# Loading two weight matrices through casting DMAs from GpSimd instead of staged loads and engine casts, with batch 1's loads held back by a gate

## The chip, the core and the metric

The kernel runs on one core of a Trainium2 chip. The metric is the device time of one execution in microseconds (us), given as the median of several runs. The engines are TensorE (PE, with its weight loads as PEld), VectorE (DVE), ScalarE (ACT), GpSimd (POOL) and SyncE (SP, which here only issues DMAs). Each engine works through its own instructions in order and waits for others by semaphores. Sixteen DMA engines move data between HBM and SBUF.

## The reference

A retention layer over eight batches (batch 8, heads 8, sequence 576, head size 64) is followed by a two-layer network with a tanh-gelu. All inputs and the output are float32.

```python
scores = (1 / sqrt(64)) * q @ k.transpose(0, 1, 3, 2)
gamma = 1 - 2.0 ** (-5 - arange(H))
Dmat = where(rel >= 0, gamma ** rel, 0)          # rel = row position - column position
x = (scores * Dmat) @ v                          # then to [4608 tokens, 512]
h = x @ w_in                                     # w_in  512 x 2048
g = 0.5 * h * (1 + tanh(sqrt(2 / pi) * (h + 0.044715 * h**3)))
out = g @ w_out                                  # w_out 2048 x 512
```

## The kernel before

The work is cut into token blocks of 512 (`TB`), nine of them: one for each batch's first 512 positions, and a last block that gathers the remaining 64 positions of all eight batches. All matmuls have float16 operands. For each batch there is an attention part (transposes, scores, masks, running states, outputs) that leaves `xT`, and a network part on `xT`: `up` matmuls with `w_in_sb` into PSUM, the gelu on ScalarE into `gT`, and `prod` matmuls with `w_out_sb` and with sums of its quarters (`wt`, made by VectorE at L764). The order of all instructions is written out by hand: the emission order in the program is each engine's order, and `at(t, u, f)` hangs a piece of work `f` on step `u` of block `t`. Negative steps of block 0 lie in its `up` part. While block 0's network part runs, batch 1's attention is slotted in, and so on.

At the start, batch 0's twelve loads of q, k and v go through SP into ten staging buffers (`lds`, float32, 128 by 512 each, freed by `unstage`). `cc` casts a staged tile to float16 on a chosen engine, frees its buffer, and calls `pump`, which issues the next loads in the list `seq` as long as buffers are free. An entry `("h",)` in `seq` stops `pump` until `resume` is called.

After batch 0 the list holds 16 loads of `w_in` (L121) and 16 of `w_out` (L126), each 256 KB, and then batch 1's loads. `w_in` comes in four column groups of 512 in the order `QS = (0, 2, 1, 3)`, each as four chunks of 128 rows (`ct`); `w_out` in sixteen chunks of 128 rows. `cast_w` (its cast is L921) casts the staged chunks into `w_in_sb` and `w_out_sb`: all of `w_in` and chunks 0 to 9 of `w_out` on GpSimd, chunks 10 to 15 on ScalarE (`BY_ACT`).

PE's order at the start is: batch 0's attention; `up_halves` on column group 0; the rest of batch 0's outputs; then fourteen more `up_half` steps of eight matmuls each (L614), groups 0 and 2 first and then 1 and 3; then the products of block 0 (L802): product 1 (opA, w_out chunks 0 to 7), product 5 (opC), product 2 (opA again, chunks 8 to 11 and then 12 to 15), products 3, 6, 7 and 4 with batch 1's attention among them. Batch 1's casts of q and k for the first half run on VectorE (L292), of v on GpSimd (L280); its q is turned at step 8 of block 0.

Of the kernel before, what the change touches and what calls it, by code (L numbers as in the profile page):

```python
# [20 lines left out]
def kernel(  # L21
# [9 lines left out]
    nc = tc.nc  # L31
# [8 lines left out]
    NF = DF // 128  # L40
# [20 lines left out]
    def bank(name, dt=F32):  # L61
        n = spare.popleft()
        t = ps.tile([128, 512 if dt == F32 else 1024], dt, tag=f"p{n}", name=name, bufs=1)
        home[id(t)] = (n, t)
        return t

    def drop(t):
        spare.append(home.pop(id(t))[0])
# [4 lines left out]
    def lds(name="ld", shape=(128, 512), dt=F32):  # L73
        n = stage.popleft()
        t = sb.tile(list(shape), dt, tag=f"ld{n}", name=name, bufs=1)
        staged[id(t)] = (n, t)
        return t

    def unstage(t):
        if id(t) in staged:  # L80
            stage.append(staged.pop(id(t))[0])
# [19 lines left out]
    def load(b, key, c):  # L101
        src = SRC[key]
        t = lds()
        if b < NPE or key == "q":
            g, y = c // 2, c % 2
            nc.sync.dma_start(
                out=t.rearrange("p (n x) -> p n x", n=4),
                in_=src[b, y::2, 256 * g : 256 * g + 256, :].rearrange("n (p j) d -> p n (j d)", j=2),
            )
        else:  # L110
            nc.sync.dma_start(
                out=t.rearrange("p (h d) -> p h d", d=D),
                in_=src[b, :, 128 * c : 128 * c + 128, :].rearrange("h s d -> s h d"),
            )
        att[b]["raw"][key, c] = t

    w_raw = {}

    def load_w_in(g, ct):
        t = lds()  # L120
        nc.sync.dma_start(out=t, in_=moe_w_in[128 * ct : 128 * ct + 128, 512 * g : 512 * g + 512])  # L121
        w_raw["i", g, ct] = t

    def load_w_out(f):
        t = lds()
        nc.sync.dma_start(out=t, in_=moe_w_out[128 * f : 128 * f + 128, :])  # L126
        w_raw["o", f] = t

    def parts(b):
        if b == NPE:  # L130
            return [(key, c) for key in "kqv" for c in range(NC)]
        return [(key, c) for c in range(NC) for key in "kqv"]

    def body(b):
        if b < NPE:
            return [("b", b, key, 2 * g + y) for g in range(2) for key in "qkv" for y in range(2)]
        return [("b", b, *x) for x in parts(b)]

    QS = (0, 2, 1, 3)
    seq = body(0) + [("i", g, ct) for g in QS for ct in range(4)]  # L140
    seq += [("o", f) for f in range(NF)] + body(1)
    TP = {4: 0, 5: 2, 6: 4, 7: 6}
    for b in range(1, B):
        seq += body(b) if b > 1 else []
# [6 lines left out]
    def pump():  # L151
        while q_ld["next"] < len(seq) and not q_ld["hold"]:
            s = seq[q_ld["next"]]
            if s[0] == "h":
                q_ld["hold"] = True
                q_ld["next"] += 1
                return
            if s[0] != "t":
                if not stage:
                    return  # L160
            q_ld["next"] += 1
            {"b": load, "i": load_w_in, "o": load_w_out, "t": load_tails}[s[0]](*s[1:])

    pump()


# [22 lines left out]
    for n in range(2):  # L189
# [3 lines left out]
            out=lp[:, 32 + 16 * n : 48 + 16 * n].rearrange("p (x h) -> p x h", h=8),  # L193
# [50 lines left out]
    w_in_sb = const.tile([128, 4, DF], F16, name="w_in_sb")  # L244
    w_out_sb = const.tile([128, NF, DM], F16, name="w_out_sb")
# [3 lines left out]
    def filler(n, w=512):  # L249
        t = bank("fill")  # L250
        for _ in range(n):
            for x in range(0, 512, w):
                nc.tensor.matmul(t[:, x : x + w], ident, wide[:, x : x + w], start=(x == 0), stop=True, skip_group_check=True)
        drop(t)
# [17 lines left out]
    def cast(b, key, c, eng):  # L272
        a = att[b]
        raw = a["raw"].pop((key, c))
        dst = a[key][:, 512 * c : 512 * c + 512]
        if key == "v":
            if eng is nc.scalar:
                eng.copy(out=dst, in_=raw)  # L278
            else:
                eng.tensor_copy(out=dst, in_=raw)  # L280
        elif key == "q" and NPE <= b < PAIR:
            g, y = c // 2, c % 2
            for x in range(2):
                eng.tensor_tensor(  # L284
                    out=a[key][:, 1024 * g + 512 * x : 1024 * g + 512 * x + 512].rearrange("p (n l d) -> p l n d", l=2, d=D)[:, y ^ x],
                    in0=raw[:, 256 * x : 256 * x + 256].rearrange("p (n d) -> p n d", d=D),
                    in1=sp[key][:, 4 * x : 4 * x + 4, y].unsqueeze(2).to_broadcast([128, 4, D]),
                    op=ALU.mult,
                )
        elif b < NPE:  # L290
            y = c % 2
            eng.tensor_tensor(  # L292
                out=a[key][:, 1024 * (c // 2) : 1024 * (c // 2) + 1024].rearrange("p (n l d) -> p l n d", l=2, d=D)[:, y],
                in0=raw.rearrange("p (n d) -> p n d", d=D),
                in1=sp[key][:, :, y].unsqueeze(2).to_broadcast([128, 8, D]),
                op=ALU.mult,
            )
        else:
            s0 = {"q": 0, "k": 2}[key] + (b >= PAIR)
            dh, rh = (x.rearrange("p (h d) -> p h d", d=D) for x in (dst, raw))  # L300
            for o, i in ((slice(0, 4), slice(0, 4)), (slice(4, 8, 2), slice(5, 8, 2)), (slice(5, 8, 2), slice(4, 8, 2))):
                x = rh[:, i]
                eng.tensor_tensor(  # L303
                    out=dh[:, o], in0=x, in1=sc[:, s0, i].unsqueeze(2).to_broadcast(list(x.shape)), op=ALU.mult
                )
# [31 lines left out]
    def resume():  # L337
        q_ld["hold"] = False
        pump()
# [185 lines left out]
    def past2(b, c):  # L525
        xs = bank("xs")
        att[b]["xs", c] = xs
        if c > 0:
            for p in range(HP):
                nc.tensor.matmul(  # L530
                    xs[:, 128 * p : 128 * p + 128], tbd[b % 2][:, c - 1, p, :], tq(b, c, p),
                    start=(p == 0), stop=True, skip_group_check=True,
                )
# [371 lines left out]
            drop(op.pop("B"))  # L905
            send(keep["o1"], 1)

    CP = {"i": 0, "o": 0}

    def cast_w(kind, *i):  # L910
        src = w_raw.pop((kind,) + i)
        if kind == "i":
            g, ct = i
            dst = w_in_sb[:, ct, 512 * g : 512 * g + 512]
        else:
            dst = w_out_sb[:, i[0], :]
        n = CP[kind]
        late = kind == "o" and n in BY_ACT
        eng = nc.scalar.copy if late else nc.gpsimd.tensor_copy
        CP[kind] += 1  # L920
        eng(out=dst, in_=src)  # L921
        unstage(src)
        pump()

    HALF = (2, 6)
    BY_ACT = range(10, 16)

    def cc(b, key, c, eng):
        raw = att[b]["raw"][key, c]
        cast(b, key, c, eng)  # L930
        unstage(raw)
        pump()
# [4 lines left out]
    def later(b, c, cp=None):  # L937
        scan(b, c) if b < NPE else scan_halves(b, c, cp=cp or A.copy)
        spread(b, c, cp or A.copy)
# [19 lines left out]
    for x in range(2):  # L959
        masks2(0, 0, x)  # L960
        if x == 0:
            later(0, 0)
    cc(0, "q", 2, P), cc(0, "q", 3, P)
    cc(0, "k", 2, P), cc(0, "k", 3, V)
    cc(0, "v", 2, A), cc(0, "v", 3, P)
    filler(6)
    past2(0, 0), past2(0, 1)
    av2(0, 0)
# [8 lines left out]
    for x in range(2):  # L977
        masks2(0, 1, x)
        if x == 0:
            later(0, 2)  # L980
    for g in QS:
        for ct in range(4):
            cast_w("i", g, ct)
    up_halves(0, 0, (0, 2))
    past2(0, 2), past2(0, 3)
    av2(0, 1)
# [6 lines left out]
    def at(t, u, f, last=False):  # L993
        events.setdefault((t, u, last), []).append(f)
# [22 lines left out]


    at(0, -12, lambda: V.memset(tbd[1][:, 1:], 0.0))
    for f in range(NF):  # L1020
        at(0, (f - 10) // 2 if f in BY_ACT else -7 + f // 2 if f < 8 else -1, lambda f=f: cast_w("o", f))
    for u, f, ns in ((-4, 0, (0,)), (-1, 4, (0,)), (2, 0, (1, 2)), (4, 4, (1, 2))):
        at(0, u, lambda f=f, ns=ns: weight_sums(f, ns, V))
    for u, f, e in ((6, 0, V), (6, 4, V)):
# [106 lines left out]
    for t in range(1, B):  # L1131
        b, tl = t + 1, TP.get(t)
# [12 lines left out]
    for b in range(NPE, B):  # L1145
        ent = parts(b)
        eng = {"k": P, "q": P, "v": P if b == NPE + 1 else A}
# [121 lines left out]
```

## Time and profile before

| | |
|---|---|
| runs shown, us | 282.88, 284.13, 284.18 (median 284.13) |
| profiled execution, us | 283.43 |
| its span, us | 281.7 |
| TensorE clock granted | 0.997 of full |
| PE, DVE, ACT, POOL busy, us | 271.3, 234.8, 170.4, 137.3 |
| read from and written to HBM, MB | 36.70, 9.44 |
| w_in load, issue to landing, us (median) | 5.9 |
| w_out load, issue to landing, us (median) | 5.3 |

The profile is of one execution. Its span runs from the first to the last instruction; the time of the execution holds 1.7 us more. Timeline lines give start, duration, engine, line, operation, output and input, a count where like instructions are merged, and in brackets the idle time before and what ended it. Rows by stage give for each engine its busy time and count of instructions, then the granted TensorE clock, the mean busy share of the DMA engines and GB/s. "SPq" is SP's queue of DMA issues.

### The profile page before, as it was taken

To read this page: it belongs to the slowest core of one execution; us is meant where nothing else is said; L and a number is where in the kernel's file an instruction comes from. 1 tells how busy PE (TensorE), PEld (TensorE's weight loads), DVE (VectorE), ACT (ScalarE), POOL (GpSimd) and SP (SyncE) were. 2 spreads that over 40 slices of the span, in tenths; PEclk is the share of its full clock that TensorE was granted. 3 is DMA by queue.
4 is the path that set the end of the run, shared out by engine and by line. 5 is a ranking of instruction groups with operands and counts; after the bars stand their busy time and mean duration, and the time that the engine had idled before them with its cause. 6 is when DMAs were issued, how large, how long until landed. Compare 5 with 4: busy or idle time off the path is not lost.

```text
span 281.7 us, 9782 instructions
## 1 busy us (share of the span) xinstructions
PE 271.3 (96%) x4106; PEld 214.2 (76%) x4106; DVE 234.8 (83%) x441; ACT 170.4 (60%) x325; POOL 137.3 (49%) x239
## 2 busy tenths in 40 slices
PE   6789999999999999999999999999999999999994
PEld 3458887888877688768876886688668887887783
DVE  6784999998979799779988997889798977975874
ACT  5377755797336864785468745884587358407810
POOL 5579909890596089108961797169817000000000
PEclk9999999999999999999999999999999999999998
DMA  6999999999998994999699989999992240003005
GB/s 187 304 376 341 388 307 259 232 198 243 248 221 156 284 223 95 258 239 238 126 199 282 210 186 189 282 212 195 193 269 44 40 153 1 2 31 120 0 7 144
DMA packets 127307, 54.11 MB, mean 192 GB/s; under 512 B 93472, under 2 KB 119072, under 8 KB 127264
## 3 DMA queue, kind: packets, MB, share of 16 engines
q1 hardware_dynamic: 126672, 52.97, 77.3%
q8 instruction: 32, 0.52, 0.8%
q10 hardware_dynamic: 592, 0.52, 0.5%
q14 instruction: 11, 0.09, 0.1%
HBM read 36.70 MB, written 9.44 MB: 164 GB/s over the span
## 4 chain that ended last, share of the span: by engine, by line
PE 70%; DVE 13%; DMA 6%; ACT 4%; POOL 3%; issue 2%; SPq 1%; DVEq 0%
PE hp L593 11%; PE opB L802 11%; PE opA L802 10%; PE opC L802 8%; PE hB L695 8%; PE opD L802 4%; DMA ld<-in_moe_w_in_dram 4%; PE hC L695 4%; PE xs L428 3%; PE hp L614 3%; DVE wt L764 2%; ACT gT L710 2%; DMA ld<-in_v_dram 2%; POOL w_in_sb L921 2%; PE hA L695 2%
## 5 line engine op out<-in xcount | busy, mean ns | idle before, releaser
L802 PEld LDWEIGHTS <-gT 128*128 128x128 f16 x576 | 55.0, 98 | 8.7 <-issue 0.2
L593 PE MATMUL hp<-xT,w_in_sb 128*128 128x512 f16 x192 | 49.1, 379 | 0.0
L802 PEld LDWEIGHTS <-s 128*128 128x128 f16 x432 | 42.0, 98 | 5.1
L303 POOL TENSOR_TENSOR ck<-ld,sc 128x128 f16<-128x128 f32 (+1 forms) x72 | 43.3, 628 | 2.9 <-DMA ld<-in_k_dram 2.5
L599 ACT ACTIVATE gT<-hp 128x512 f16<-128x512 f32 x48 | 28.5, 594 | 11.0 <-PE hp L593 10.9
L802 PE MATMUL opA<-w_out_sb,gT 128*128 128x256 f16 x288 | 35.0, 273 | 0.0
L284 POOL TENSOR_TENSOR cq<-ld,sc 128x256 f16<-128x256 f32 x48 | 32.1, 690 | 0.0
L695 PEld LDWEIGHTS <-w_in_sb 128*128 128x128 f16 x256 | 25.1, 98 | 8.2
L614 PE MATMUL hp<-xT,w_in_sb 128*128 128x256 f16 x256 | 29.8, 273 | 1.5 <-POOL w_in_sb L921 1.3
L614 PEld LDWEIGHTS <-w_in_sb 128*128 128x128 f16 x256 | 24.2, 98 | 5.8 <-POOL w_in_sb L921 2.8
L593 PEld LDWEIGHTS <-w_in_sb 128*128 128x128 f16 x192 | 18.7, 98 | 12.8 <-DVE xT L579 0.2
L710 ACT ACTIVATE gT<-k 128x512 f16<-128x512 f32 x25 | 15.8, 632 | 13.1 <-DVE k L706 13.1
L695 PEld LDWEIGHTS <-wi 128*128 128x128 f16 x192 | 18.3, 98 | 5.2
L621 ACT ACTIVATE gT<-hp 128x512 f16<-128x512 f32 x32 | 18.5, 599 | 4.8 <-PE hp L614 4.7
L1157 POOL COPY gate<-s 128x1 f16<-128x1 f16 x5 | 2.5, 496 | 38.4 <-DVE s L777 30.9
L776 DVE TENSOR_TENSOR s<-gT 128x512 f16<-128x512 f16 (+1 forms) x26 | 14.7, 566 | 7.7 <-ACT gT L621 5.0
L579 ACT CAST xT<-xs 128x512 f16<-128x512 f32 x23 | 15.3, 734 | 8.7 <-PE xs L428 8.7
L695 PE MATMUL hC<-x,w_in_sb 128*128 128x256 f16 x128 | 19.2, 273 | 0.0
L695 PE MATMUL hB<-x,wi 128*128 128x256 f16 x128 | 18.9, 273 | 0.0
L802 PE MATMUL opB<-wt,gT 128*128 128x256 f16 x144 | 18.2, 273 | 0.0
L278 ACT CAST cv<-ld 128x512 f16<-128x512 f32 x22 | 13.7, 622 | 7.4 <-DMA ld<-in_v_dram 7.4
L779 DVE TENSOR_TENSOR gT<-gT 128x512 f16<-128x512 f16 (+1 forms) x26 | 18.1, 712 | 0.0
(150 smaller groups left out, 569.3 us busy)
## 6 DMA issues: line engine op xcount, KB each, us to landing
ld<-in_q_dram SPq DMA_DIRECT2D x32, 256.0 KB, 5.6
ld<-in_k_dram SPq DMA_DIRECT2D x32, 256.0 KB, 5.7
ld<-in_v_dram SPq DMA_DIRECT2D x32, 256.0 KB, 5.6
out_dram<-ost SPq DMA_DIRECT2D x16, 512.0 KB, 4.7
ld<-in_moe_w_in_dram SPq DMA_DIRECT2D x16, 256.0 KB, 5.9
ld<-in_moe_w_out_dram SPq DMA_DIRECT2D x16, 256.0 KB, 5.3
lt<-in_k_dram SPq DMA_DIRECT2D x8, 128.0 KB, 5.9
lt<-in_q_dram SPq DMA_DIRECT2D x8, 128.0 KB, 4.5
```

Source lines behind the costliest of these rows:

```text
L284: eng.tensor_tensor(out=a[key][:, 1024 * g + 512 * x : 1024 * g + 512 * x + 512].rearrange("p (n l d) -> p l n d", l=2, d=D)[:, y ^ x], in ...
L303: eng.tensor_tensor(out=dh[:, o], in0=x, in1=sc[:, s0, i].unsqueeze(2).to_broadcast(list(x.shape)), op=ALU.mult)
L579: cp(out=xT[:, g0 : g0 + 4 : 2].rearrange("p g n (t j) -> p g n j t", j=2), in_=t.rearrange("p (n g j t) -> p g n j t", n=HP, g=2, j=2),)
L593: nc.tensor.matmul(hp.rearrange("p (g t) -> p g t", t=TL), w_in_sb[:, ct, 128 * fc : 128 * fc + 128], xT[:, o : o + TB // TL, ct, :], star ...
L599: nc.scalar.activation(out=gT[t][:, fc].rearrange("p i n -> p (i n)"), in_=hp, func=AF.Gelu_apprx_tanh)
L614: nc.tensor.matmul(hps[n][:, 256 * x : 256 * x + 256].rearrange("p (g t) -> p g t", t=TL), w_in_sb[:, ct, 128 * (fs[n] + x) : 128 * (fs[n] ...
L621: nc.scalar.activation(out=gT[t][:, f : f + 2, 2 * u : 2 * u + 2, :].rearrange("p f i n -> p f (i n)"), in_=hp.rearrange("p (f n) -> p f n ...
L695: nc.tensor.matmul(pb[:, 256 * i : 256 * i + 256].rearrange("p (g t) -> p g t", t=TL), w(kt, i), x(kt), start=(new and i == kt == 0), stop ...
L710: due.append(lambda: nc.scalar.activation(out=g, in_=x.rearrange("p (f n) -> p f n", f=2), func=AF.Gelu_apprx_tanh))
L776: nc.vector.tensor_tensor(out=s["1"], in0=a21, in1=a22, op=ALU.add)
L779: nc.vector.tensor_tensor(out=a21, in0=a11, in1=a21, op=ALU.subtract)
L802: nc.tensor.matmul(op[tag][:, HD * u : HD * u + HD], lhs(f), rhs[:, f], start=(new and f == 0), stop=(f == NH - 1), skip_group_check=True,)
```

## The change

Both weight matrices are no longer staged. Nine DMAs issued from GpSimd read the float32 weights from HBM and write float16 straight into `w_in_sb` and `w_out_sb`: group 0 of `w_in` in two halves of 512 KB, the other three groups in 1 MB each, and `w_out` in four quarters of 1 MB. The issues stand in GpSimd's order among batch 0's second-half casts. All 32 staged weight loads on SP, and the 26 casts on GpSimd and six on ScalarE, are taken out.

Batch 1's loads now follow batch 0's in `seq`, behind a hold that is lifted at step -9 of block 0. The first of them must wait for a new one-column copy on GpSimd, which reads chunk 11 of `w_out` (the last of its third quarter) and writes into the buffer that this load fills. In the built program the copy waits for the eighth of the nine DMAs, and the ninth DMA waits for the first, whose semaphore it uses again.

```diff
     def load(b, key, c):
         t = lds()
+        if (b, key, c) == (1, "q", 0):
+            nc.gpsimd.tensor_copy(out=t[:, 0:1], in_=w_out_sb[:, 11, 0:1])
...
-    def load_w_in(g, ct):
-        t = lds()
-        nc.sync.dma_start(out=t, in_=moe_w_in[128 * ct : 128 * ct + 128, 512 * g : 512 * g + 512])
-        w_raw["i", g, ct] = t
-
-    def load_w_out(f):
-        t = lds()
-        nc.sync.dma_start(out=t, in_=moe_w_out[128 * f : 128 * f + 128, :])
-        w_raw["o", f] = t
+    def load_w_in(g, c0, c1):
+        nc.gpsimd.dma_start(
+            out=w_in_sb[:, c0:c1, 512 * g : 512 * g + 512],
+            in_=moe_w_in[128 * c0 : 128 * c1, 512 * g : 512 * g + 512].rearrange("(c p) f -> p c f", p=128),
+        )
+
+    def load_w_out(f0, f1):
+        nc.gpsimd.dma_start(
+            out=w_out_sb[:, f0:f1], in_=moe_w_out[128 * f0 : 128 * f1, :].rearrange("(f p) d -> p f d", p=128)
+        )
...
-    seq = body(0) + [("i", g, ct) for g in QS for ct in range(4)]
-    seq += [("o", f) for f in range(NF)] + body(1)
+    seq = body(0) + [("h",)] + body(1)
...
     cc(0, "q", 2, P), cc(0, "q", 3, P)
+    load_w_in(0, 0, 2)
     cc(0, "k", 2, P), cc(0, "k", 3, V)
+    load_w_in(0, 2, 4)
     cc(0, "v", 2, A), cc(0, "v", 3, P)
+    load_w_in(2, 0, 4)
+    load_w_in(1, 0, 4)
+    load_w_in(3, 0, 4)
+    load_w_out(0, 4)
+    load_w_out(4, 8)
+    load_w_out(8, 12)
+    load_w_out(12, 16)
     filler(6)
...
-    for g in QS:
-        for ct in range(4):
-            cast_w("i", g, ct)
     up_halves(0, 0, (0, 2))
...
-    for f in range(NF):
-        at(0, (f - 10) // 2 if f in BY_ACT else -7 + f // 2 if f < 8 else -1, lambda f=f: cast_w("o", f))
+    at(0, -9, resume)
```

`cast_w`, `BY_ACT` and `w_raw` are removed with their uses.

More of the change, by code (lines that the diff above doesn't have):

```diff
@@ L115, in load @@
         att[b]["raw"][key, c] = t
-    w_raw = {}
-    def load_w_in(g, ct):
-        t = lds()
-        nc.sync.dma_start(out=t, in_=moe_w_in[128 * ct : 128 * ct + 128, 512 * g : 512 * g + 512])
-        w_raw["i", g, ct] = t
-    def load_w_out(f):
-        t = lds()
-        nc.sync.dma_start(out=t, in_=moe_w_out[128 * f : 128 * f + 128, :])
-        w_raw["o", f] = t
+    def load_w_in(g, c0, c1):
[7 more added lines that the diff above has]
+        )
     def parts(b):
@@ L161, in pump @@
             q_ld["next"] += 1
-            {"b": load, "i": load_w_in, "o": load_w_out, "t": load_tails}[s[0]](*s[1:])
+            {"b": load, "t": load_tails}[s[0]](*s[1:])
     pump()
@@ L906, in after @@
             send(keep["o1"], 1)
[L908 to L923, printed above, removed]
     HALF = (2, 6)
-    BY_ACT = range(10, 16)
     def cc(b, key, c, eng):
```

## The prediction

> **What bounds the kernel now.** I read the page's busy shares first, then the busy time by stage, then the timeline of the start and the waits there.
>
> ```profile
> span 281.7 us, 9782 instructions
> ...
> PE 271.3 (96%) x4106; PEld 214.2 (76%) x4106; DVE 234.8 (83%) x441; ACT 170.4 (60%) x325; POOL 137.3 (49%) x239
> ```
>
> TensorE (PE) is busy in 96% of the span, so 10.4 us of idle time are all that better loading could win. The stages show where they are.
>
> ```profile
> core 0: us, PE busy (x) PEld busy (x) DVE busy (x) ACT busy (x) POOL busy (x), PEclk, DMA share, GB/s
> ...
> 12.30:16.50 4.20, 3.54 (x119) 2.63 (x119) 3.64 (x8) 3.14 (x8) 1.59 (x2) 1.00 1.08 355
> 16.50:22.00 5.50, 4.08 (x60) 2.52 (x61) 4.08 (x9) 3.60 (x8) 5.11 (x8) 1.00 1.05 374
> 22.00:34.00 12.00, 12.00 (x111) 10.75 (x112) 8.37 (x12) 8.66 (x17) 11.65 (x17) 1.00 1.01 362
> 34.00:41.70 7.70, 7.70 (x73) 6.88 (x71) 7.60 (x14) 4.87 (x9) 1.47 (x2) 1.00 1.13 320
> 41.70:50.70 9.00, 8.36 (x174) 7.17 (x173) 8.93 (x16) 5.25 (x7) 7.42 (x9) 1.00 1.05 249
> ```
>
> After 22 us PE is full, but for 0.64 us at 41.7 to 50.7, where batch 1's attention is slotted in. The weights stream from about 12 to 38 us with the 16 DMA engines saturated (share 1.0 or more) at 362 to 374 GB/s. In 16.5 to 22.0 PE waits for weights:
>
> ```profile
> 10.13 11.66 SPq L121 DMA_DIRECT2D ld<-in_moe_w_in_dram  x16
> ...
> 12.23 1.05 POOL L292 TENSOR_TENSOR ck<-ld,sc 128x512 f16<-128x512 f32 x1
> ...
> 14.69 0.61 POOL L280 CAST cv<-ld 128x512 f16<-128x512 f32 x1 [1.41 <-DMA ld<-in_v_dram]
> ...
> 16.55 5.33 POOL L921 CAST w_in_sb<-ld 128x512 f16<-128x512 f32 x8 [1.25 <-DMA ld<-in_moe_w_in_dram]
> ...
> 17.22 1.28 PE L614 MATMUL hp<-xT,w_in_sb 128*128 128x256 f16 x8 [0.76 <-POOL w_in_sb L921]
> ...
> 20.83 0.78 PE L614 MATMUL hp<-xT,w_in_sb 128*128 128x256 f16 x3
> ...
> 21.93 8.25 PE L614 MATMUL hp<-xT,w_in_sb 128*128 128x256 f16 x74 [0.33 <-POOL w_in_sb L921]
> ```
>
> The eight casts at 16.55 are column groups 0 and 2 of w_in. PE starts at 17.22 on the first, follows them chunk by chunk, and only from 21.93 runs without a stop. Its work from 16.5 to 21.93 is 19 matmuls of L614 at 0.109 us (0.87 us for eight) and 1.1 us of attention, 3.2 us in 5.4: about 2.2 us are lost here. That and the 0.64 us are the ceiling of any gain.
>
> ```profile
> 33.25 1.13 SPq L106 DMA_DIRECT2D ld<-in_q_dram  x2
> ...
> 33.84 1.91 PE L802 MATMUL opA<-w_out_sb,gT 128*128 128x256 f16 x16
> ...
> 37.37 1.91 PE L802 MATMUL opA<-w_out_sb,gT 128*128 128x256 f16 x16
> ```
>
> These set the later deadlines: in chunks of 128 rows, the first opA needs chunks 0 to 7 of w_out, the second chunks 8 to 11 at 37.37 and 12 to 15 eight matmuls later, at 38.24. Batch 1's first load leaves SP at 33.25.
>
> **What goes.** 26 casts on POOL (16 of w_in, median 0.62 us, and ten of w_out, median 0.80) and six on ACT (0.62) fall away. PE waited only for the first eight, priced below; the rest ran beside a full PE, so they are worth nothing in themselves. VectorE's sums beside them take 0.71 to 0.83 us (L777 to L781) and 0.42 once POOL is quiet, but VectorE there waits for gelus. SP loses 32 issues and 8.4 MB of staged loads.
>
> **What comes: the issues.** GpSimd issues in order, so nine issues of cost c stand in its queue: one between the casts of q3 and k2, one between k2 and v3, seven behind v3. No row shows a DMA issued from POOL. Nearest below: SP's w_in issue of 128 rows, 0.33 us at the least. From above: SP's longest batch-0 or batch-1 q issue (512 rows, as in seven of the nine), 1.34 us. A cost below zero is excluded, since POOL must at least step through the instruction. I take 0.8 us, between the two and equal to POOL's own median for a w_out cast. k2 then ends at 13.28+0.8 = 14.1 (PE turns k at 14.10, so it hardly notices), v3 at 15.5 in place of 15.3 (PE's state matmuls want it at 16.0). At c = 1.34 v3 ends at 16.6, and PE's attention is 0.6 us late.
>
> In one sentence of its own: the Trainium skill (DMA: Bandwidth & Descriptors, Latency and other measured facts) gives about 1 us to the first byte for a GpSimd DMA against 0.6 for one of SP, which no run here shows yet, and by an estimate from it each landing would be 0.4 us later.
>
> **The transfers.** I take the old stream's rate, 370 GB/s of float32 read: 1 MB in 2.83 us. Landing after the last byte: batch 0's first load, issued at 0.81 into an idle queue, released VectorE at 3.85; less 0.46 of issue and 0.7 of transfer that leaves 1.8 us. With c = 0.8: group 0's halves flow from 13.1 and 14.9 and land at 16.3 and 18.2; group 2 is issued by 16.3 and lands at 21.0. Before, PE had 3 of its 8 matmuls done when it resumed at 21.93, as if it had started at 21.6. So 0.6 us are won here (1.3 us at c = 0.33; 1.0 us lost at 1.34). Groups 1 and 3 land at 23.8 and 26.7, wanted at 26.2 and 28.0. The quarters of w_out land at 29.5, 32.3, 35.2 and, undisturbed, 38.0; PE wants them at 33.2, 33.2, 36.8 and 37.6. VectorE's weight sums (L764) began at 30.93, 34.91, 37.39 and 38.72, one for each quarter, so they too meet their data but for the last.
>
> The last is late. The gate opens at 35.2 and batch 1's loads then share the engines with the last quarter: at half rate for it, 38.9. PE stops 1.3 us there, and 0.6 won becomes 0.7 lost.
>
> **The gate.** The one-column copy waits on POOL for w_out chunk 11. Behind it there stand only batch 1's casts of v, q and k, whose data it holds back anyway; on SP all of batch 1's loads stand behind q's first. Before, these began at 33.25 and took until 43.7 (SP waited for staging buffers); now ten go without a buffer wait from 35.3. Into the shared engines, q lands at 38.8 and 39.5, k at 40.2 and 40.9, v at 41.6 and 42.3; before, with 5.5 us from issue to landing, 38.8, 39.4, 40.3 and so on, v released POOL at 42.23. VectorE's casts of q began at 40.05. So batch 1 is at most some tenths late. Of the 0.7 us, 0.2 vanish into PE's 0.64 us of idle time.
>
> **Sum.** The profiled execution took 283.43 us (span 281.7 and 1.7 around it); +0.5 gives 283.9. The median of the runs shown is 284.13, 0.7 above it, so on that scale 284.6. About 0.5%, 1.4 us, is what a measurement of this kernel can tell from no change.
>
> **Rivals.**
>
> *Converting in flight is slower than copying* (25%). Nothing in the trace converts inside a DMA. For it: the engines are already saturated at 370 GB/s, and the last quarter has no slack (38.0 against 37.6), so every loss of rate reaches PE. Against it: the bytes read are the same and those written are half. It decides from a rate of about 355 GB/s, where 8.4 MB take 1 us longer. At 90% the stream is 2.5 us longer (287), at 75% 7.6 us (292), at half rate 22.7 us (307).
> The Trainium skill (DMA: Bandwidth & Descriptors, Bandwidth, Measured) lists 341 GB/s for 1 MB from GpSimd; by an estimate from that the stream takes 24.6 us in place of 22.7 and the sum is 1.9 us higher, 286.5. The old stream's 374 GB/s is from SP, so the trace neither agrees nor disagrees.
>
> *The issues are dear* (18%): c at 1.34 us or more, or a first issue of several us. Place: POOL between q3 and v3. All landings move by three issues, 1.6 us at c = 1.34: w_out's last quarter at 40.5, 2.3 us late; 286 to 287. It decides from c = 1.1.
>
> *Faster* (20%): issues of 0.33 us and a stream above 400 GB/s because half as much is written. Group 2 lands before 20.0, PE resumes 1.5 us or more earlier, and w_out's last quarter, 2 us earlier, no longer stops it: 282.0 to 282.7. The ceiling of 2.2+0.64 us speaks against much more. For it: 18 us of POOL's casts really are gone, and PE waited 4.1 us for them by the waits:
>
> ```profile
> PEld L614 <- POOL w_in_sb L921: 2.8, 6, 0.9
> ...
> PE hp L614 <- POOL w_in_sb L921: 1.3, 3, 0.8
> ```
>
> (weight loads and matmuls count the same stops twice.) Against it: those casts ran almost as fast (0.62 us for 256 KB) as the transfers do (0.71 us), so what replaces them is the DMA's own pace.
>
> *No change beyond 1.4 us* (37%) is the forecast. That the gate does not hold is excluded: q's load writes the column that the copy writes, so it must follow it.
>
> **The numbers.** Near zero 0.37, slower 0.43 (25+18), faster 0.20. The faster case reaches down to 282.0. Upward the range takes the dear issues and the milder half of the slow stream, to 84% of its rate (4.3 us on top of 0.5), 289; beyond lie about 13%.
>
> **What would show it.** Right: PE's unbroken run of L614 begins near 21.0; a POOL issue takes 0.5 to 1.1 us; a short stop at the second opA; batch 1's q casts begin at 40 to 40.5; everything after 60 us is as before but shifted. Wrong: DMA busy with less than 340 GB/s from 15 to 36 us, or PE waiting for w_out by several us (slow stream); k2's cast after 15 us (dear issues); w_out's third quarter before 33 us (faster).

## The result and the profile after

The changed kernel takes 285.20 us (median of nine runs, 284.92 to 287.72), the kernel before, beside it and over nine runs, 283.52: a ratio of 1.0065, 95% interval 1.0040 to 1.0091. That is 1.8 us slower by the ratio, past the 0.5%, 1.4 us, that the prediction named as what can be told from no change. The profiled execution took 285.1 us, of which 283.4 are span (before: 283.43 and 281.7).

From the page after: the span, the engines' busy times and the two DMA queues that matter (packets, MB, share of 16 engines).

```profile
span 283.4 us, 9700 instructions
...
PE 271.6 (96%) x4106; PEld 215.2 (76%) x4106; DVE 231.3 (82%) x441; ACT 167.4 (59%) x319; POOL 125.6 (44%) x223
...
q1 hardware_dynamic: 122064, 44.58, 68.8%
q0 software_dynamic: 4240, 4.19, 9.3%
```

PE's work is the same (271.6 us against 271.3), VectorE and GpSimd have 3.5 and 11.7 us less to do, and the span is longer all the same. The software queue's 4.19 MB are the float16 bytes written of both weights. So where it alone is at work, the GB/s of the stages below are written bytes, and the float32 read is twice that.

Busy time by stage, after:

```profile
core 0: us, PE busy (x) PEld busy (x) DVE busy (x) ACT busy (x) POOL busy (x), PEclk, DMA share, GB/s
...
12.30:16.50 4.20, 3.19 (x90) 2.31 (x94) 4.03 (x6) 2.69 (x6) 4.18 (x6) 1.00 0.75 133
16.50:22.00 5.50, 3.56 (x68) 2.74 (x56) 4.59 (x10) 2.93 (x7) 4.08 (x6) 0.85 0.95 136
22.00:34.00 12.00, 11.55 (x129) 10.15 (x128) 4.42 (x11) 8.35 (x16) 0.00 (x0) 0.93 1.24 207
34.00:41.70 7.70, 7.70 (x73) 6.90 (x72) 6.26 (x14) 2.81 (x6) 0.19 (x1) 1.00 0.99 215
41.70:50.70 9.00, 8.92 (x177) 7.77 (x174) 8.28 (x15) 4.25 (x6) 5.92 (x7) 1.00 1.12 274
```

From 22 to 34 us the new stream runs at 207 GB/s written, 414 read, faster than the old one's 362. From 16.5 to 22 us it runs at 136 written, some 270 read, where the old one had 374. The stage before, with 133 in place of 355, still holds the last of batch 0's plain loads. PE's idle time moved with that: 1.94 us in 16.5 to 22.0 (before 1.42) and 0.45 in 22 to 34 (before none), while 41.7 to 50.7 is nearly full (8.92, before 8.36). PEclk is 0.85 and 0.93 in the two stages, so some of PE's busy time there is work at half speed.

GpSimd's timeline after shows the issues (L120, L126) and the gate (L105):

```profile
12.15 0.89 POOL L120 DMA_DIRECT2D w_in_sb<-in_moe_w_in_dram  x1
...
14.06 0.76 POOL L120 DMA_DIRECT2D w_in_sb<-in_moe_w_in_dram  x1
...
15.37 2.24 POOL L120 DMA_DIRECT2D w_in_sb<-in_moe_w_in_dram  x3
17.59 2.99 POOL L126 DMA_DIRECT2D w_out_sb<-in_moe_w_out_dram  x4
36.48 0.19 POOL L105 CAST ld<-w_out_sb 128x1 f32<-128x1 f16 x1 [15.91 <-issue]
```

An issue takes 0.75 to 0.89 us. PE's timeline after:

```profile
16.87 1.03 PE L614 MATMUL hp<-xT,w_in_sb 128*128 128x256 f16 x8
19.85 1.42 PE L614 MATMUL hp<-xT,w_in_sb 128*128 128x256 f16 x8 [1.94 <-DMA w_in_sb<-in_moe_w_in_dram]
...
23.57 12.49 PE L614 MATMUL hp<-xT,w_in_sb 128*128 128x256 f16 x112 [0.45 <-DMA w_in_sb<-in_moe_w_in_dram]
35.89 1.91 PE L802 MATMUL opA<-w_out_sb,gT 128*128 128x256 f16 x16
...
39.39 1.91 PE L802 MATMUL opA<-w_out_sb,gT 128*128 128x256 f16 x16
```

The first eight matmuls run at 16.87, as soon as the first half is there. Then PE stands for 1.94 us for the second half, and the unbroken run begins at 23.57 on group 2, where the kernel before had an equivalent start of 21.6. Both opA steps are 2.0 us later than before (33.84, 37.37). Neither stops for w_out.

One row per us, in the same columns, shows the slow stretch (the trace's landing records give group 0's halves at 16.4 and 19.8, group 2 at 23.5):

```profile
15.00:16.00 1.00, 1.00 (x11) 0.47 (x8) 0.86 (x3) 0.74 (x2) 1.00 (x2) 1.00 0.85 128
16.00:17.00 1.00, 1.00 (x67) 0.93 (x67) 0.97 (x3) 1.00 (x3) 1.00 (x3) 1.00 0.82 105
17.00:18.00 1.00, 0.90 (x8) 0.56 (x6) 1.00 (x3) 0.54 (x2) 1.00 (x2) 1.00 0.70 79
18.00:19.00 1.00, 0.00 (x0) 0.00 (x0) 0.97 (x3) 0.28 (x1) 1.00 (x2) 1.00 0.75 96
...
22.00:23.00 1.00, 1.00 (x34) 0.82 (x32) 0.00 (x0) 0.00 (x0) 0.00 (x0) 0.50 1.24 213
```

Three things stand in these rows: a written rate of 79 to 128 GB/s until 19 us and above 200 from 22 us on, PE without work from 18 us, and a granted clock of one half at 22 us (by the rows left out, from 20.4 to 23.8). The experiments take them up in turn.

### The profile page after: what moved, and what is told of

It reads as the page before. It is cut to its first block, busy times and chain, and to the rows that moved or that the text cites. A ratio compares the mean times of both kernels' runs of the same rounds, so it can differ in the third digit from the quotient of the medians.

```text
span 283.4 us, 9700 instructions
## 1 busy us (share of the span) xinstructions
PE 271.6 (96%) x4106; PEld 215.2 (76%) x4106; DVE 231.3 (82%) x441; ACT 167.4 (59%) x319; POOL 125.6 (44%) x223
## 3 DMA queue, kind: packets, MB, share of 16 engines
q0 software_dynamic: 4240, 4.19, 9.3%
## 4 chain that ended last, share of the span: by engine, by line
PE 81%; DMA 7%; ACT 4%; DVE 3%; POOL 2%; SPq 1%; issue 1%; DVEq 0%
PE opA L802 11%; PE opB L802 11%; PE hp L593 11%; PE hp L614 9%; PE opC L802 9%; PE hB L695 8%; PE opD L802 5%; PE hC L695 4%; PE xs L428 3%; DMA w_in_sb<-in_moe_w_in_dram 3%; DMA ld<-in_q_dram 2%; DMA tt<-cq 2%; ACT gT L710 2%; PE hA L695 2%; PE opE L802 2%; PE us L428 1%
## 5 line engine op out<-in xcount | busy, mean ns | idle before, releaser
L614 PE MATMUL hp<-xT,w_in_sb 128*128 128x256 f16 x256 | 29.6, 275 | 2.4 <-DMA w_in_sb<-in_moe_w_in_dram 2.4
L614 PEld LDWEIGHTS <-w_in_sb 128*128 128x128 f16 x256 | 24.7, 98 | 6.0 <-DMA w_in_sb<-in_moe_w_in_dram 2.9
L593 PEld LDWEIGHTS <-w_in_sb 128*128 128x128 f16 x192 | 18.7, 98 | 12.8 <-DVE xT L579 0.2
L710 ACT ACTIVATE gT<-k 128x512 f16<-128x512 f32 x25 | 15.8, 631 | 13.0 <-DVE k L706 13.0
L695 PEld LDWEIGHTS <-wi 128*128 128x128 f16 x192 | 18.3, 98 | 5.1
L695 PE MATMUL hC<-x,w_in_sb 128*128 128x256 f16 x128 | 19.2, 273 | 0.0
L802 PE MATMUL opB<-wt,gT 128*128 128x256 f16 x144 | 18.2, 273 | 0.0
L802 PE MATMUL opB<-wt,s 128*128 128x256 f16 x144 | 17.4, 273 | 0.0
## 6 DMA issues: line engine op xcount, KB each, us to landing
w_out_sb<-in_moe_w_out_dram POOLq DMA_DIRECT2D x4, 512.0 KB, 16.4
```

Of the source, the lines that this page charges most:

```text
L593: nc.tensor.matmul(hp.rearrange("p (g t) -> p g t", t=TL), w_in_sb[:, ct, 128 * fc : 128 * fc + 128], xT[:, o : o + TB // TL, ct, :], star ...
L614: nc.tensor.matmul(hps[n][:, 256 * x : 256 * x + 256].rearrange("p (g t) -> p g t", t=TL), w_in_sb[:, ct, 128 * (fs[n] + x) : 128 * (fs[n] ...
L695: nc.tensor.matmul(pb[:, 256 * i : 256 * i + 256].rearrange("p (g t) -> p g t", t=TL), w(kt, i), x(kt), start=(new and i == kt == 0), stop ...
L710: due.append(lambda: nc.scalar.activation(out=g, in_=x.rearrange("p (f n) -> p f n", f=2), func=AF.Gelu_apprx_tanh))
L802: nc.tensor.matmul(op[tag][:, HD * u : HD * u + HD], lhs(f), rhs[:, f], start=(new and f == 0), stop=(f == NH - 1), skip_group_check=True,)
```

## The experiments

Four kernels take on the first theories. *Theory 1*: GpSimd's own issuing slows the stream, since the slow stretch ends about when the last issue does (20.6 us). *Theory 2*: the software queue's first use costs a start-up.

**Hold the rest.** The six issues after group 2's wait for group 2:

```diff
     load_w_in(2, 0, 4)
+    landed(0, w_in_sb[:, 3, 1535:1536])    # a one-column copy on GpSimd that reads group 2's last column
     load_w_in(1, 0, 4)
```

> The changed kernel, but a one-column copy on POOL waits for w_in group 2 before the last six DMAs are issued. Theory 1 (while POOL issues DMAs, the casting stream runs at about half its pace): after POOL's third issue, at about 16 us, the DMAs write about 200 GB/s as they do after 21 us in the changed kernel, group 2 lands at 20 to 21 us in place of 23.5, and PE's L614 run resumes then; a hole in the DMA traffic and a second slow stretch of about 5 us follow behind the copy, and w_out's last quarter lands at 41 to 43. Theory 2 (the first 7 us of a casting stream are slow, whatever POOL does): group 2 lands at 23 to 24 as in the changed kernel, and the six DMAs issued afterwards run at full pace at once.

One execution: 290.24 us. Its rows per us, first in the early stretch and then after the second burst of issues, which begins at 23.55 us:

```profile
17.00:18.00 1.00, 0.69 (x7) 0.38 (x4) 1.00 (x3) 0.33 (x1) 0.00 (x0) 1.00 0.72 67
18.00:19.00 1.00, 0.00 (x0) 0.00 (x0) 0.97 (x4) 0.48 (x2) 0.00 (x0) 1.00 0.86 117
...
24.00:25.00 1.00, 1.00 (x12) 0.90 (x10) 0.00 (x0) 0.50 (x1) 1.00 (x2) 1.00 0.01 1
25.00:26.00 1.00, 1.00 (x12) 0.90 (x10) 0.00 (x0) 0.70 (x2) 1.00 (x3) 1.00 0.92 35
26.00:27.00 1.00, 1.00 (x11) 0.90 (x10) 0.96 (x3) 0.60 (x1) 1.00 (x2) 1.00 1.23 204
```

GpSimd issued nothing from 15.9 to 23.5 us, and the stream was as slow as before; group 2 landed at 23.4 and the run began at 23.42. Theory 1 falls. The second burst shows a start-up with nothing else on the engines: almost no data until 25 us, 35 GB/s in the next microsecond, 204 in the one after, so about 1.5 us from the begin of the issue to the first data and 2.5 to the full rate. Most of the 5 us over the changed kernel are PE's waits for groups 1 and 3 and for w_out: it waits 4.4 us for w_in and 1.8 for w_out, against 2.4 and none.

**Warm the queue.** A 32 KB casting DMA into a spare tile at about 2 us:

```diff
+    primed = const.tile([128, 64], F16, name="primed")
+    nc.gpsimd.dma_start(out=primed, in_=moe_w_in[0:128, 0:64])
```

> The changed kernel with one small extra casting DMA (32 KB, into a tile that nobody reads) issued from POOL at about 2 us, when POOL waits for its first load. Theory 1 (issuing slows the stream): nothing changes, group 2 lands at 23 to 24 us, 285 us. Theory 2 (the software queue's first use is slow): the slow stretch at 13 to 20 us disappears, group 2 lands near 21, 283 to 284 us.

One execution: 286.72 us; the slow rows are unchanged (105, 117, 104 and 86 GB/s from 15 to 19 us) and the run begins at 23.55. Theory 2 falls.

**Many issues.** w_out in sixteen DMAs in place of four:

```diff
-    load_w_out(0, 4)
-    load_w_out(4, 8)
-    load_w_out(8, 12)
-    load_w_out(12, 16)
+    for f in range(NF):
+        load_w_out(f, f + 1)
```

> The changed kernel with w_out in sixteen DMAs of 256 KB in place of four of 1 MB: the same bytes, twelve more issues on POOL (0.7 to 0.8 us each), at most eight in flight. Theory 1 (issuing slows the stream): the DMAs write 100 to 150 GB/s until the last issue, w_out's last chunk lands after 43 us, PE waits several us at the second opA; 288 us or more. Theory 2 (only the start is slow): w_out's last chunk at 39 to 40 us as in the changed kernel, 285 to 286 us.

One execution: 285.96 us. GpSimd was still issuing at 34 us. The rows have 200 to 214 GB/s from 20 to 31 us, so issues beside the stream cost nothing there. From 31 to 36 us four of five rows have 169 to 198; PE did not wait for w_out.

**Two in flight.** By such copies, each issue from the fourth on waits until the DMA three before it has landed, so that two others are in flight when it is issued. (What was expected speaks of the DMA "two before it"; the edit waits for the third before.)

```diff
     load_w_in(2, 0, 4)
+    landed(0, w_in_sb[:, 1, 0:1])
     load_w_in(1, 0, 4)
...
```

> The changed kernel, with each 1 MB issue from w_in group 1 on held on POOL (one-column copies) until the DMA two before it has landed, so that the issues are spread over the stream and two transfers are always in flight. Theory 1 (issuing slows the stream while it lasts): group 2 lands at about 21 us in place of 23.5, PE's L614 run is unbroken from there, w_out's last quarter lands at 38.5 to 40; 283 to 284 us, 1.5 to 2 us under the changed kernel and within 0.5% of the kernel before. Theory 2 (slow start): group 2 at 23 to 24 us, all later landings as in the changed kernel or later; 285 to 286 us.

Measured 286.04 us, a ratio of 1.0094 (1.0062 to 1.0126). Group 2 landed at 23.4, the run began at 23.45, rows of 90 to 111 GB/s from 15 to 19 us: no gain, against theory 1 once more. Rows of 139 to 194 GB/s come back from 27 to 32 us, with no more than three pieces in flight.

*Theory 3* came next: the queue runs empty. A half of group 0 is 1.3 us of data at 400 GB/s, but the halves are issued 1.9 us apart, with k2's cast between them, and group 2 behind v3's cast; each time the queue is dry when the next issue's start-up is over. Its rival: the stretch is slow by what lies beside it (batch 0's last loads, the engines' work), whatever is queued.

**One burst.** Group 0 as one DMA, and group 2 right behind it:

```diff
     cc(0, "q", 2, P), cc(0, "q", 3, P)
-    load_w_in(0, 0, 2)
+    load_w_in(0, 0, 4)
+    load_w_in(2, 0, 4)
     cc(0, "k", 2, P), cc(0, "k", 3, V)
-    load_w_in(0, 2, 4)
     cc(0, "v", 2, A), cc(0, "v", 3, P)
-    load_w_in(2, 0, 4)
```

> Group 0 of w_in comes as one 1 MB DMA in place of two halves, and it and group 2 are issued one behind the other after q3's cast, ahead of the casts of k2 and v3 (which so start about 0.8 us later). Theory 3 (the stream starts up anew whenever the queue has run empty, and the halves with casts between them let it run empty twice): issues at 12.15 and 12.9; written data reach 200 GB/s by about 15 us and stay there; group 0 lands by 17.5, group 2 at 20 to 20.6 in place of 23.5; the unbroken L614 run begins at 20.2 to 20.8, about 1 us before the equivalent start of the kernel before; 282.5 to 283.5 us. Rival (the stretch from 13.5 to 19.5 us is slow by its neighbourhood, whatever is queued): the slow slices stay, group 2 lands at 23 to 24, the run begins at 23.3 or later, 285 to 286 us.

Measured 283.30 us, a ratio of 1.0001 (0.9980 to 1.0022). Its rows, and PE's timeline:

```profile
14.00:15.00 1.00, 0.12 (x3) 0.08 (x3) 0.73 (x1) 0.86 (x2) 1.00 (x2) 1.00 0.69 69
15.00:16.00 1.00, 1.00 (x11) 0.58 (x11) 0.42 (x2) 0.64 (x2) 1.00 (x2) 1.00 1.23 204
```

```profile
17.84 1.92 PE L614 MATMUL hp<-xT,w_in_sb 128*128 128x256 f16 x16 [0.83 <-DMA w_in_sb<-in_moe_w_in_dram]
...
20.71 12.40 PE L614 MATMUL hp<-xT,w_in_sb 128*128 128x256 f16 x112
32.95 1.91 PE L802 MATMUL opA<-w_out_sb,gT 128*128 128x256 f16 x16
```

The stretch that the rival holds to be slow whatever is queued runs at 202 to 208 GB/s from 15 to 20 us. Group 2 landed at 20.3, the run begins at 20.71, opA at 32.95: 2.9 us ahead of the changed kernel, 0.9 ahead of the one before. The rival falls. The loss against the kernel before is gone, but the lead of 0.9 us did not show in the time; the span is 0.4 us shorter than before, within what single executions differ by.

**The burst sooner**, and **ahead of q2.** As above, with group 0's issue between the casts of q2 and q3, or ahead of both:

```diff
+    load_w_in(0, 0, 4)                 # ahead of q2; in the other kernel between q2 and q3
     cc(0, "q", 2, P), cc(0, "q", 3, P)
-    load_w_in(0, 0, 2)
+    load_w_in(2, 0, 4)
     cc(0, "k", 2, P), cc(0, "k", 3, V)
-    load_w_in(0, 2, 4)
     cc(0, "v", 2, A), cc(0, "v", 3, P)
-    load_w_in(2, 0, 4)
```

> As the kernel with one burst, but group 0 is issued between the casts of q2 and q3, group 2 right behind q3's. Theory 3: data begin about 0.8 us earlier, as batch 0's last loads end (about 13 us), no empty queue between the two; group 2 at 19.3 to 20, the L614 run from 19.5 to 20.3, 282 to 283 us unless v3 lands late. Rival (slow by neighbourhood): group 2 still at 23 or later, 285 to 286 us.

> Group 0's one DMA is issued before q2's cast (about 9.9 us), so that it shares the engines with batch 0's last loads; group 2 behind q3's cast. Theory 3: group 0 lands by 16 but batch 0's k2 and v3 land up to 2.5 us later, PE's attention of batch 0 is late by 1 to 2 us and the L614 run begins at 20 to 21.5: 282.5 to 284.5 us. Rival (slow by neighbourhood): group 0's data are moved before the slow stretch, group 2 still lands at 22 to 23.5, 284.5 to 286 us.

Sooner: 282.97 us, 0.9986 (0.9962 to 1.0010); rows of 128 to 189 GB/s from 15 to 20 us, group 2 at 20.2, the run at 20.34. Ahead of q2: 282.42 us, 0.9983 (0.9956 to 1.0010); 199 GB/s or more in every row from 13 to 20 us, group 2 at 19.4, the run at 20.17, opA at 32.40:

```profile
16.00:17.00 1.00, 0.70 (x58) 0.59 (x48) 1.00 (x3) 0.99 (x4) 1.00 (x2) 1.00 1.24 206
17.00:18.00 1.00, 1.00 (x11) 0.89 (x10) 0.97 (x3) 0.23 (x1) 1.00 (x3) 1.00 1.25 206
```

```profile
20.17 12.40 PE L614 MATMUL hp<-xT,w_in_sb 128*128 128x256 f16 x112
32.40 1.91 PE L802 MATMUL opA<-w_out_sb,gT 128*128 128x256 f16 x16
```

Batch 0's loads came no later (its last landed by 14.2, in the changed kernel by 14.4), so the feared contention cost nothing that shows. This is the lowest median found; its interval still holds 1, so it is not shown to be faster than the kernel before.

**The gate at half.** The changed kernel with the gate on chunk 7:

```diff
-            nc.gpsimd.tensor_copy(out=t[:, 0:1], in_=w_out_sb[:, 11, 0:1])
+            nc.gpsimd.tensor_copy(out=t[:, 0:1], in_=w_out_sb[:, 7, 0:1])
```

> The changed kernel with the gate on chunk 7 of w_out (half of it) in place of chunk 11. The gate opens about 2.6 us earlier, at 33.8 in place of 36.4, batch 1's loads share the engines with half of w_out. If the gate costs nothing, as the changed kernel's cast of q (40.85, no wait for a DMA) says: 285.2 us within 0.3, and PE may stop at the second opA for w_out up to 1 us. If the gate made batch 1 late (ck waits of 0.33 and 0.21 us): up to 0.5 us less.

Measured 288.08 us, 1.0105 (1.0057 to 1.0154), which neither reading foresaw. The executions come in two groups, 284.7 to 285.1 and 288.1 to 289.3. The profiled one (288.61) is of the second, and its rows tell why:

```profile
21.00:22.00 1.00, 1.00 (x25) 0.80 (x26) 0.35 (x1) 0.94 (x2) 0.00 (x0) 0.58 1.25 207
22.00:23.00 1.00, 0.66 (x28) 0.42 (x16) 0.00 (x0) 0.30 (x1) 0.00 (x0) 0.50 1.25 214
...
27.00:28.00 1.00, 1.00 (x7) 0.67 (x5) 0.46 (x2) 0.47 (x1) 0.00 (x0) 0.51 1.24 207
```

The granted clock was 0.50 from 21.2 to 28.0 us, before the gate does anything, and the unbroken run of 112 matmuls took 14.70 us in place of 12.49. The gate opened at 33.88 in place of 36.48, and no wait for w_out appeared. So the gate is worth less than 0.5 us by the first group. The second group has the lower clock: the mean granted clock is 0.987 to 0.994 in its four executions and 0.994 to 1.000 in the three of the first. In the profiled one the fall cost 1.9 of 3.5 us by the first opA (37.78 against 35.89); the rest was not traced.

**Fill the pause.** Dummy matmuls (the kernel's `filler`) in PE's two pauses for w_in, eight ahead of the second eight of L614 and five ahead of the run:

```diff
-    def up_halves(t, u, fs):
+    def up_halves(t, u, fs, pad=0):
...
         for ct, n, x in some if len(fs) > 1 else sorted(some, key=lambda s: s[2]):
+            if pad and (ct, n, x) == (2, 0, 0):
+                filler(pad)
...
-    up_halves(0, 0, (0, 2))
+    up_halves(0, 0, (0, 2), 8)
     past2(0, 2), past2(0, 3)
     av2(0, 1)
+    filler(5)
```

> The changed kernel with 13 dummy matmuls (the kernel's own filler, 128x512, 0.24 us each) in PE's two pauses for w_in: eight ahead of the second eight of L614, five ahead of the unbroken run. The loads are untouched, so the run begins at 23.4 to 23.8 as before. If the pause of 1.9 us is what lets the granted clock fall: it stays at 1.00 from 18 to 30 us, no execution goes over 286.3 us, median 284.8 to 285.3. If the clock falls for another reason: 0.5 still shows in some stretch between 20 and 28 us, and some executions take 286.5 to 289 as in the changed kernel and in the kernel with the earlier gate.

Measured 285.64 us, 1.0060 (1.0037 to 1.0083). In the profile the clock stayed at 1.00 in every row from 12 to 30 us, also in what were PE's pauses, and the run began at 23.60:

```profile
18.00:19.00 1.00, 1.00 (x7) 0.46 (x5) 0.97 (x4) 0.05 (x1) 1.00 (x2) 1.00 0.93 95
22.00:23.00 1.00, 1.00 (x24) 0.50 (x13) 0.00 (x0) 0.85 (x3) 0.00 (x0) 1.00 1.26 205
```

All eight executions have a mean granted clock of 0.997 or more, where four of the changed kernel's nine have 0.992 to 0.994. The slowest took 286.48, 0.2 over the bound set, but none took the 287.7 to 289 of the other two kernels. The pause lets the clock fall, then; and the clock is not what made the changed kernel slower, since the ratio stays.

**Halves together**, and **one gap.** Two kernels tell the size of the pieces from the gaps. In the first the two halves and group 2 are issued one behind the other after q3's cast. In the second group 0 is one DMA, but group 2 stays behind v3's cast:

```diff
     cc(0, "q", 2, P), cc(0, "q", 3, P)
     load_w_in(0, 0, 2)
+    load_w_in(0, 2, 4)
+    load_w_in(2, 0, 4)
     cc(0, "k", 2, P), cc(0, "k", 3, V)
-    load_w_in(0, 2, 4)
     cc(0, "v", 2, A), cc(0, "v", 3, P)
-    load_w_in(2, 0, 4)
```

```diff
-    load_w_in(0, 0, 2)
+    load_w_in(0, 0, 4)
     cc(0, "k", 2, P), cc(0, "k", 3, V)
-    load_w_in(0, 2, 4)
     cc(0, "v", 2, A), cc(0, "v", 3, P)
     load_w_in(2, 0, 4)
```

> Group 0 again in two halves of 512 KB, as in the changed kernel, but both and group 2 are issued one behind the other after q3's cast, with no cast between them. The size of a piece and the gap between the issues are told apart. If the gaps cost the time (the queue runs empty between the issues): the stream is at 195 GB/s written or more by 16 us and stays there, group 2 lands at 20.3 to 20.8, the unbroken L614 run begins at 20.5 to 21.2, 282.7 to 284 us. If the small pieces cost it: slices of 80 to 130 GB/s between 15 and 19 us as in the changed kernel, the run from 23 us, 285 or more.

> Group 0 as one DMA of 1 MB in the place of its first half, group 2 behind v3's cast as in the changed kernel: the size of the kernel with one burst, but one gap (issues at 12.1 and about 15.5). If gaps cost the time: group 0 at 17.5 to 17.8; group 2's issue ends at 16.4, when group 0's data end too, so the rate dips once at 16.5 to 18.5 and group 2 lands at 20.8 to 21.8, the run begins at 21 to 22, 283.5 to 284.7 us. If the size of the pieces alone mattered: no dip, group 2 at 20.3, the run as with one burst, 283 us.

Halves together, one execution: 285.67 us, but not for the loads:

```profile
16.00:17.00 1.00, 1.00 (x9) 0.72 (x7) 0.31 (x1) 0.74 (x2) 1.00 (x3) 0.50 1.23 204
17.00:18.00 1.00, 1.00 (x11) 0.16 (x13) 0.87 (x3) 0.89 (x3) 1.00 (x2) 0.50 1.08 159
18.00:19.00 1.00, 1.00 (x52) 1.00 (x52) 0.45 (x1) 0.75 (x2) 1.00 (x2) 0.50 1.24 202
```

```profile
15.66 0.99 PE L321 MATMUL tr<-ident,ck 128*128 128x128 f16 x8 [1.37 <-POOL ck L292]
...
19.26 1.92 PE L614 MATMUL hp<-xT,w_in_sb 128*128 128x256 f16 x16
...
22.44 12.40 PE L614 MATMUL hp<-xT,w_in_sb 128*128 128x256 f16 x112
```

PEclk stands ahead of the DMA share, GB/s last. The stream is at 204 GB/s from 16 us, with one dip; the halves landed at 16.5 and 18.3, group 2 at 21.0. Small pieces by themselves do not make the stretch slow. One thing differs beside the gap: VectorE, busy in nearly all of 15 to 20 us in the changed kernel, was mostly idle here from 15 to 17 us (0.06 and 0.31). Also, three issues ahead of k2's cast (it starts at 14.54) made PE wait 1.37 us for it, the clock fell to 0.50 from 15.8 to 19.2 us, batch 0's attention ran at half pace, and PE came to L614 only at 19.26, with the weights waiting for it.

One gap, one execution: 284.57 us. Group 2's issue ended 2.9 us behind group 0's, against 2.6 us of data. The rows dip to 163 and 161 GB/s at 16 to 18 us; group 2 landed at 20.2 and the run began at 20.25, sooner than theory 3's 21 to 22. One piece of 1 MB in place of two halves is enough for most of the gain, with a gap behind it. opA, at 32.49, is 1.35 us ahead of the kernel before, yet the span is 1.2 longer (282.9). Part of that is in the waits of PE after 60 us:

```profile
PE us L428 <- POOL cv L280: 0.7, 1, 0.7
PE st L428 <- DMA tt<-cq: 0.6, 1, 0.6
```

L428 belongs to later batches' attention, and `tt<-cq` is a transposing DMA; the kernel before has no such wait after 60 us. Of the kernels that start early, one burst and the burst sooner have none, ahead of q2 has 0.8 us. Before 60 us PE waited 0.9 us for batch 1's k, whose load VectorE had waited for as long. That makes 2.2 us of waits behind the first opA, where the kernel before has 0.7 (0.3 for k, 0.4 for a sum of VectorE). The rest of the 2.5 us was not traced; it is one execution.

**k2 ahead of group 2.** The kernel with group 0 ahead of q2, with group 2's issue moved behind k2's cast:

```diff
     load_w_in(0, 0, 4)
     cc(0, "q", 2, P), cc(0, "q", 3, P)
-    load_w_in(2, 0, 4)
     cc(0, "k", 2, P), cc(0, "k", 3, V)
+    load_w_in(2, 0, 4)
     cc(0, "v", 2, A), cc(0, "v", 3, P)
```

> As the kernel that issues group 0 before q2's cast, with group 2's issue moved behind k2's cast, ahead of v3's: PE's wait of 0.7 us for k2's cast on POOL should go. Group 2's issue then ends at about 14.2, while group 0's data still flow (until about 15.5), so the rate dips little: group 2 at 19.4 to 20.4, the L614 run from 20.0 to 20.6, 282.0 to 282.8 us, a ratio of 0.997 to 0.999 to the kernel before. If the gap counts here too: a dip to 130 GB/s at 15.5 to 16.5, group 2 at 21, 283 to 283.6 us.

Measured 284.89 us, 1.0027 (0.9997 to 1.0058). The issues now end 3.8 us apart against 2.6 us of data, and the gap shows: 170 and 138 GB/s at 15 to 17 us, group 2 at 20.9 in place of 19.4, the run at 20.91 after a wait of 0.50. The wait of 0.7 us for k2's cast on GpSimd gave way to one of 0.48 for k3's on VectorE; the gap cost more at the run's start (0.74 us). The executions spread from 282.17 to 286.61 with the clock at 0.997 or more, which nothing here explains.

Side by side, with the issues by their ends:

| kernel | what the queue sees | group 2, us | run, us |
|---|---|---|---|
| changed | two halves 1.8 us apart, group 2 1.3 us on | 23.5 | 23.57 |
| hold the rest; two in flight | the same start | 23.4 | 23.42; 23.45 |
| halves together | no gap, halves | 21.0 | 22.44 (PE itself late) |
| k2 ahead of group 2 | 1 MB, then 3.8 us | 20.9 | 20.91 |
| one burst | 1 MB, then 0.7 us | 20.3 | 20.71 |
| burst sooner | 1 MB 1.4 us sooner, then 1.8 us | 20.2 | 20.34 |
| one gap | 1 MB, then 2.9 us | 20.2 | 20.25 |
| ahead of q2 | 1 MB 2.6 us sooner, then 2.8 us | 19.4 | 20.17 |

It is shown that the order and size of the first issues make the loss: with short pieces and casts between their issues the stretch is slow, and either remedy, more data in one piece or no gap, takes most of it away (halves together and one gap in one execution each). That the queue runs dry between the issues, theory 3, is not shown. The trace's records of single packets (1 KB of float16 each) speak partly for it and partly against it.

For it: in the changed kernel most packets take as long in the slow stretch as later, 98 ns, but there are fewer of them, 86 a us from 16 to 18.5 us against 199 from 22 to 30. The DMA engines stand part of the time without a packet; an ordinary packet is not slower.

Against it: the second half was issued by 14.8 us, and 2.5 us from the begin of that issue end at 16.6. Yet its data were moved from 15.7 to 18.7, 3.0 us for what takes 1.3 at the later rate, and group 2, issued by 16.1, began only then. (This counts packets in the order of issue.) Each DMA ends with 16 packets of 4 bytes. Those of the second half lie between 17.0 and 19.5 us, those of one burst's group 0 between 16.9 and 17.4, so the sixteen shares end far apart, and the piece lands with the last of them. Some packets take 0.3 to 1.4 us, nearly all of them before 20 us. Such packets also stand where a stream begins: 0.5 to 0.9 us at 25.1 to 25.3 in the kernel that holds the rest, 0.3 to 1.0 at 13.9 to 14.4 with one burst; with group 0 ahead of q2 there are none.

What held the second half back stays open. So does why the burst issued sooner still had rows of 128 and 164 GB/s, with 1 MB pieces 1.8 us apart (group 2 landed at 20.2, theory 3 asked for 19.3 to 20). A rival that no run tests is that work on VectorE or GpSimd beside an issue holds the issued piece back: in the changed kernel the rate reaches 200 GB/s just after VectorE's work ends (21.3 us). One burst has the same VectorE work from 16 to 20 us at 202 to 208 GB/s, but both of its pieces had been issued by 13.8.

## Why the prediction was right, and where it was not

The forecast of 284.6 us lies 0.6 below the measured 285.2, inside its range. That it came so near is in part luck: it stood on a median of 284.13 for the kernel before, which over nine runs is 283.52. The difference was missed: +0.5 us forecast, +1.8 measured, beyond the 1.4 us of the case that was forecast (37%), and by another route than the one told. Of the signs named for being right, the cost of an issue came (0.75 to 0.89 us); the run of L614 near 21.0, the stop at the second opA and the q casts by 40.5 did not.

- **Issues.** Taken at 0.8 us between 0.33 and 1.34; measured 0.75 to 0.89. k2's cast ended at 14.1 and v3's at 15.4, as worked out. The dear issues fell.
- **The steady rate.** Taken at 370 GB/s read; measured 404 to 426 in the rows from 22 to 30 us, 2.5 us per MB. The slow conversion did not come, and the rate is the one that the faster case needed. The prediction read a DMA share of 1.0 or more as saturated; it goes to 1.2 here. The old stream's 362 from 22 to 34 us is not its pace either: its rows have 389 to 404 GB/s from 26 to 30 us, and 266 to 326 from 22 to 26, and SP's issues waited 4.1 us for earlier loads and casts from 20 to 27 us. The Trainium skill (DMA: Bandwidth & Descriptors, Measured) has 341 GB/s for a 1 MB load from GpSimd; the runs here, with several loads queued and half the bytes written, are above it, and the 286.5 by that figure is above the measured time.
- **The first landings.** This is the step that failed: group 0's halves "land at 16.3 and 18.2; group 2 is issued by 16.3 and lands at 21.0", and "0.6 us are won here". Measured 16.4, 19.8 and 23.5, and 2.0 us lost. The step let each piece flow at the old stream's full rate from the end of its issue: 1.4 us for a half. The second half took 3.0, and group 2's data began at 18.7 in place of 16.3. The old stream had 16 issues of 256 KB from an engine with nothing else to do; nothing in its rows priced pieces issued between casts. With one burst, group 2 beats the step's own figure (20.3), so the issues are the cause; why they slow the stream stays open, as said above.
- **w_out's last quarter.** Its landing, 38.9, came out to the tenth by luck (a later start and a higher rate cancelled); the stop of 1.3 us did not. PE was 2.0 us late itself and wanted the second half of that step at 40.3.
- **The gate.** It opened at 36.5 and cost little: batch 1's q casts began at 40.85, behind VectorE's own sums and not behind a load; k waited 0.33 and 0.21 us. "At most some tenths" held, and the kernel with the earlier gate gave no more.
- **What is absorbed.** 0.2 us of idle time at 41.7 to 50.7 was to swallow part of the loss; 0.3 of the 2.0 us vanished by the span (+1.7).
- **The faster case** asked for group 2 before 20.0 and PE 1.5 us or more earlier, for 282.0 to 282.7. The kernel with group 0 ahead of q2 has group 2 at 19.4, opA 1.4 us earlier and 282.42 us, which its interval does not tell from the kernel before. The change as written doesn't reach it.

## What to carry to other kernels

When loads move to an engine that also has casts on the critical path, its program order feeds the DMA queue. What worked here was 1 MB in the first piece (2.5 us of data, about as long as the 1.5 to 2.5 us from an issue to its data), or issues back to back; short pieces between casts lost 2 us. It did not always reach the full rate: with 1 MB pieces 1.8 or 3.8 us apart rows of 128 to 189 GB/s remained. Don't price such pieces at the rate of a steady stream. Then count who waits behind the issues, since three in a row cost PE 1.4 us and a clock drop. A gain at the start of a kernel that is bound by one engine shows in the time only as far as later waits, in one of the kernels here transposing DMAs and batch 1's loads, don't take it back.

## What the runs showed of the hardware

- A DMA that converts float32 to float16 ran at 414 GB/s read over 12 us, against 362 of plain loads in the same stretch of the kernel before, whose rows run from 266 to 404 and whose issues waited for earlier loads and casts. So it is not shown that the converting DMA is the faster kind.
- After pauses of 1.4 to 2.0 us in PE's work the granted clock fell to one half in five profiles (changed, warm queue, many issues, gate at half, halves together) and did not in two with pauses of 2.0 and 2.4 us (hold the rest, two in flight). By the trace's clock records it stayed low for 3.41 us in four and 6.83 in one, and the stretch at full clock ahead of each fall lasted 3, 4 or 5 times 3.41 us (10.24, 13.65, 17.07). The Trainium skill (TensorE: Matmul & The Clock Gate, What's actually happening) has a free-running window of about 3.4 us: the lengths agree, and so does the chance in whether a pause is caught. Its rule of thumb that gaps must exceed about 3.4 us to matter (HAM oscillation) does not hold here: 1.4 us with sparse work around it was enough.
- Whether a fall costs anything depends on what it meets: in the changed kernel's profile it lay over attention while the weights were still coming and cost nothing at the run's start; in the kernel with the gate at half it lay over the run itself and cost 1.9 us at opA.
